# A fused attention, expert and gated-layer kernel: the embedding norm on another engine, gates and post steps at other places, a note per step in the gated layer

## The chip, the cores and the metric

The kernel runs on one core of one Trainium2 chip. The metric is the device time of one execution in microseconds (us); of several executions the median counts. The five engines of the core that appear in the profile are TensorE (PE; its weight loads, which overlap its products, are PEld), VectorE (DVE), ScalarE (ACT), GpSimd (POOL) and SyncE (SP), which issues most loads and stores.

## The reference

Three layers follow one another. The first is a recurrent attention over 4 batches, 8 heads, 768 places and 40 columns per head:

```python
for t in range(S):
    m_new = np.maximum(f_gate[:, :, t] + m, i_gate[:, :, t])
    f_stab = np.exp(f_gate[:, :, t] + m - m_new)
    i_stab = np.exp(i_gate[:, :, t] - m_new)
    m = m_new
    C = f_stab * C + i_stab * outer(v[t], k[t])
    n = f_stab * n + i_stab * k[t]
    y[:, :, t] = sigmoid(o_gate[t]) * (C @ q[t]) / np.maximum(np.abs(n @ q[t]), 1.0)
```

Its 3072 rows of 320 columns go through eight experts, of which each row takes the one with the largest logit:

```python
xn = x / (norm(x) + 1e-06)
en = expert_emb / (norm(expert_emb) + 1e-06)
logits = xn @ en.T / tau
expert_idx = np.argmax(logits, axis=1)
out[mask] = gate_w[mask, None] * (np.maximum(x[mask] @ w1[e], 0.0) @ w2[e])
```

The rows then go through a gated layer with 1536 hidden columns: `(sigmoid(x @ w_gate) * (x @ w_val)) @ w_out`. `expert_emb` has 8 rows of 320 columns; its norm, and the factor 1/tau with it, is what the change moves.

## The kernel before, in words

**Order.** The program sets the order itself: each engine runs its instructions in the order in which the code issues them, and a wait is a wait for everything behind it on that engine. `weave` issues several lists of operations in turn, one of each. `sideq` is a queue of small VectorE operations, and `side(n)` issues the next n of it at the place where it stands.

**Attention stage (to about 146 us).** There are 24 tiles, numbered from 0: tile i is chunk i // 4 (128 places) of batch i % 4. A tile passes through these steps:

- `st_S` (L428): TensorE's eight score products into two banks (`s_ps`); from tile 9 on every other tile (`HALF`) uses half of the rows only. VectorE masks both banks (`am`, and `s_ps` in place), ScalarE casts both to `ah`, GpSimd and VectorE form the remainders `al`. The first callable that it gets runs between the products and the masks, the second ahead of VectorE's `al`.
- `st_V` and `st_V2`: GpSimd scales the values with the gate column `w_all` (`vw`), ScalarE casts them to `vh`, GpSimd forms `vl`.
- `st_AV`: TensorE multiplies scores and values into bank 4 (`o_ps`); from chunk 1 on four products with the state `cst` stand ahead.
- `st_U`: TensorE's state update into bank 5 (`u_ps`); ScalarE (chunk 0) or VectorE adds it to `cst`.
- `post_ops`: VectorE's `den` (three operations) and `x`, ScalarE's sigmoid, GpSimd's product `x` and a copy.
- `st_XT` and `st_logit`: TensorE's transposes of `x` (`tp_x`), and its products with the embeddings (`l_ps`), which VectorE copies to `rs`.

The loads are issued by SyncE in the program's order; there are five buffers for keys and values (`kv`) and six for queries (`qk`), and a load waits until the tile before in its buffer is done.

**Gates.** `gate_ops(lo, hi)` is a chain of six VectorE operations on 32 rows, two of them scans; `st_gexp` takes ScalarE's exponentials, and `st_gates2` transposes both on TensorE (`tp_r`) and writes the columns `w_all` and `ri_all`. Chunk 0 has its gates ahead of tile 0, chunk 1 in the first tiles, chunks 2 to 5 together: their VectorE operations stand between tiles 5 and 8, and the exponentials and transposes of the loop's step `GX` = 5 and 6. The transposes of chunks 2 to 5 use bank 5, which the state updates use too.

**Embedding norm.** `emb_norm` squares the embeddings on ScalarE (L308), takes the root by three Newton steps on VectorE (`sqrt_ops`, L161 to L165, one column of 8 rows), and scales the embeddings on VectorE (L314). Its 15 VectorE operations come from `sideq`: `early(i)` weaves four or five of them between the post operations of the tiles 0 to 2. `emb_T` transposes the scaled embeddings after tile 5's scores.

**Filler products.** `warm(n)` issues n products of 128 x 512 ones whose result nobody reads.

**Expert stage (to about 365 us)** and **gated layer (to the end).** The gated layer runs 72 steps t, each one column block of 128 hidden columns for 512 rows. `gated_a(t)` issues the products in one half of the array's rows, gate and value products in turn into two banks; `gated_b(t)` issues those of the other halves into the same banks. So that both don't write a bank at once, `note` (L1591) lets ScalarE copy one element (`seen`) when the last product of `gated_a` is done, and `turn_rows` lets the first product of `gated_b` wait for this copy. In the steps 0 and 1 `gated_a(0)` and `gated_a(1)` are issued one after the other, and both note under the key "l1". Then ScalarE takes the sigmoid (L1622), VectorE multiplies (L1623), ScalarE casts to `hh` (L1633), GpSimd forms `hl` (L1634). `group_x` prepares the rows of the next group in three parts (`xsteps` says in which steps), each a cast on ScalarE (L209) and a subtraction on GpSimd. Beside that, pieces of weights are split on VectorE and ScalarE.

## Time and profile before

| | |
|---|---|
| three timed runs | 761.12, 763.30, 763.08 us; median 763.08 |
| the profiled execution's own time | 759.18 us, with a span of 757.4 us from its first to its last instruction |
| instructions | 17682 |
| mean granted TensorE clock | 0.993 of full speed |
| busy | PE 727.0, DVE 403.3, ACT 364.5, POOL 397.4 us |
| stages | attention to about 146 us, experts to about 365, gated layer to the end |

The rows below come from the profiled execution. In a timeline row the first number is the start in us from the span's start, the second the length in us; then come the engine, the line, the operation with its output and inputs, and how many of its kind the row merges. A bracket tells how long the engine stood idle ahead of it, and what ended that. Several short operations can overlap by their latency, so that the distance of two starts says more than the busy time.

### The profile page before, as it was taken

The numbers are of one execution on the slowest core, as the hardware profiler recorded it, in microseconds if no ns is written. First come the engines' busy times: TensorE is split into PE (matmuls) and PEld (weight loads), VectorE is DVE, ScalarE is ACT, GpSimd is POOL, SyncE is SP. The second block draws the span as 40 slices with busy tenths as digits, with TensorE's granted clock in tenths as the row PEclk, the third lists the DMA queues.
The fourth block names the chain that finished last, engine by engine and source line by source line (L and its number), as shares of the span: only waits on it lengthen the run. The fifth ranks groups of instructions, "written<-read, shape, count | busy, mean of one in ns | idle before, by whom it ended". The sixth has DMA issues, their size and how long they took to land. (4 is left out here: it accounts for less than half of the span.)

```text
span 757.4 us, 17682 instructions
## 1 busy us (share of the span) xinstructions
PE 727.0 (96%) x6906; PEld 645.3 (85%) x6906; DVE 403.3 (53%) x864; ACT 364.5 (48%) x829; POOL 397.4 (52%) x449
## 2 busy tenths in 40 slices
PE   6889999899999999999899999999999999999995
PEld 5779998799888989999688888888888888888884
DVE  7897999877778777865566664132121111111111
ACT  5765664645965656665454444333333333333322
POOL 6767887757766777886053233542324324324222
PEclk9999999999999999999999999999999999999999
DMA  7654875545455556651112210000000000000001
GB/s 221 193 160 122 265 217 162 168 119 163 146 153 160 157 158 193 185 150 53 53 57 81 81 54 19 37 35 2 1 12 27 2 1 37 1 2 35 2 1 39
DMA packets 39864, 70.46 MB, mean 93 GB/s; under 512 B 4818, under 2 KB 28460, under 8 KB 39772
## 3 DMA queue, kind: packets, MB, share of 16 engines
q1 hardware_dynamic: 36764, 59.61, 26.7%
q0 software_dynamic: 3008, 9.64, 3.9%
q8 instruction: 56, 0.92, 0.5%
q14 instruction: 36, 0.29, 0.1%
HBM read 60.55 MB, written 8.68 MB: 91 GB/s over the span
## 5 line engine op out<-in xcount | busy, mean ns | idle before, releaser
L1634 POOL TENSOR_TENSOR hl<-sgm,hh 128x512 fp32r<-128x512 f32 x71 | 95.1, 1342 | 228.5 <-ACT hh L1633 228.4
L1623 DVE TENSOR_TENSOR sgm<-v_ps,sgm 128x512 f32<-128x512 f32 (+1 forms) x73 | 49.8, 683 | 231.8 <-ACT sgm L1622 231.8
L1659 PE MATMUL o_ps<-wo,hl 64*128 64x320 f32 x560 | 87.2, 307 | 0.0
L1658 PE MATMUL o_ps<-wo,hh 64*128 64x320 f32 x560 | 86.7, 305 | 0.0
L1657 PE MATMUL o_ps<-wo,hh 64*128 64x320 f32 x560 | 86.4, 304 | 0.0
L1622 ACT ACTIVATE sgm<-g_ps 128x512 f32<-128x512 f32 (+1 forms) x73 | 43.2, 593 | 81.7 <-PE g_ps L1581 74.3
L1593 ACT COPY seen<-zeros 1x1 f32<-1x1 f32 x142 | 27.0, 190 | 105.5 <-PE v_ps L1581 57.6
L1633 ACT CAST hh<-sgm 128x512 fp32r<-128x512 f32 (+1 forms) x73 | 44.8, 615 | 48.1 <-DVE sgm L1623 47.7
L1041 ACT ACTIVATE hh<-h_ps 128x256 fp32r<-128x256 f32 (+7 forms) x72 | 35.3, 490 | 55.1 <-PE h_ps L953 50.1
L1579 PE MATMUL v_ps<-xg,wvh 64*128 64x512 f32 x144 | 56.6, 393 | 2.4 <-ACT seen L1593 2.4
L1657 PEld LDWEIGHTS o_ps<-wo,hh 64*128 64x128 f32 x560 | 53.0, 185 | 6.6 <-issue 0.3
L1658 PEld LDWEIGHTS o_ps<-wo,hh 64*128 64x128 f32 x560 | 52.8, 184 | 5.8
L1579 PE MATMUL g_ps<-xg,wgh 64*128 64x512 f32 x144 | 56.6, 393 | 0.0
L1579 PE MATMUL v_ps<-xh,wvh 64*128 64x512 f32 x144 | 56.5, 392 | 0.0
L1579 PE MATMUL g_ps<-xh,wgh 64*128 64x512 f32 x144 | 56.5, 392 | 0.0
L1580 PE MATMUL g_ps<-xg,wgh 64*128 64x512 f32 x144 | 56.4, 392 | 0.0
L1580 PE MATMUL v_ps<-xl,wvh 64*128 64x512 f32 x144 | 56.4, 392 | 0.0
L1580 PE MATMUL v_ps<-xg,wvh 64*128 64x512 f32 x144 | 56.4, 392 | 0.0
L1580 PE MATMUL g_ps<-xl,wgh 64*128 64x512 f32 x144 | 56.4, 392 | 0.0
L1581 PE MATMUL g_ps<-xg,wgl 64*128 64x512 f32 x144 | 56.2, 390 | 0.0
L1581 PE MATMUL v_ps<-xg,wvl 64*128 64x512 f32 x144 | 56.2, 390 | 0.0
L1581 PE MATMUL v_ps<-xh,wvl 64*128 64x512 f32 x144 | 56.2, 390 | 0.0
(354 smaller groups left out, 2603.8 us busy)
## 6 DMA issues: line engine op xcount, KB each, us to landing
kv<-in_kvo_dram SPq DMA_DIRECT2D x24, 484.0 KB
w2raw<-in_moe_w_dram SPq DMA_DIRECT2D x32, 320.0 KB
w1raw<-in_moe_w_dram SPq DMA_DIRECT2D x32, 256.0 KB
qk<-in_qkt_dram SPq DMA_DIRECT2D x48, 160.0 KB
xs<-x SPq DMA_DIRECT2D x24, 192.0 KB
w1raw<-in_moe_w_dram SPq DMA_DIRECT2D x64, 64.0 KB
raw<-in_moe_w_out_dram SPq DMA_DIRECT2D x12, 320.0 KB
raw<-in_moe_w_gate_dram SPq DMA_DIRECT2D x8, 384.0 KB
```

The source lines that it names most:

```text
L1041: nc.scalar.activation(out=h[f][0], in_=ps, func=AF.Relu)
L1579: lambda: nc.tensor.matmul(ps, at(wh), h[rows, kk], start=start, stop=False),
L1580: lambda: nc.tensor.matmul(ps, at(wh), l[rows, kk], start=False, stop=False),
L1581: lambda: nc.tensor.matmul(ps, at(wl), h[rows, kk], start=False, stop=stop),
L1593: passed[key] = nc.scalar.copy(seen, zeros[0:1, 0:1])
L1622: nc.scalar.activation(out=s[:, cs], in_=pg[:, cs], func=AF.Sigmoid)
L1623: nc.vector.tensor_tensor(out=s[:, cs], in0=pv[:, cs], in1=s[:, cs], op=ALU.mult)
L1633: nc.scalar.copy(gh[:, cs], s[:, cs])
L1634: e.tensor_tensor(out=gl[:, cs], in0=s[:, cs], in1=gh[:, cs], op=ALU.subtract)
L1657: lambda: nc.tensor.matmul(o, gh[rows, ts_], wh[rows], start=begin, stop=False),
L1658: lambda: nc.tensor.matmul(o, gh[rows, ts_], wl[rows], start=False, stop=False),
L1659: lambda: nc.tensor.matmul(o, gl[rows, ts_], wh[rows], start=False, stop=end),
```

## The change

- **Tile 0.** The embeddings' load is issued ahead of tile 0's keys and values. The square on ScalarE stands ahead of the first gate exponentials. VectorE's masks come ahead of the two gate columns, and the two integer operations that start the root (`norm_seed`) behind these.
- **Norm.** Of the 15 VectorE operations eleven go to GpSimd (`norm_steps`: three steps of three operations, and two more), between tile 0's `vw` and `vl`. The reciprocal stays on VectorE, between tile 1's masks and its `al`; the scaling goes to ScalarE. The transposes of the embeddings come ahead of tile 0's `tp_x`, behind tile 4's scores.
- **Post steps of tiles 0 to 3.** They are issued as the second callable of `st_S`, between the masks and `al`, not ahead of the masks.
- **Gates.** Those of chunk 1 stay where they were. Those of chunks 2 to 5 are taken from `sideq` from tile 3 on; with `GX` = 4 their exponentials and transposes come one step of the loop earlier.
- **Filler products.** Two behind the value products of tiles 1, 2 and 3, and three ahead of the first logits, where there were five.
- **Gated layer.** `note` and `turn_rows` use the step as key, a one-element sigmoid is taken ahead of step 0, and the next group's rows are prepared in the steps 2, 3 and 4, not 1, 2 and 3.

VectorE, from tile 1's `al` to tile 2's `al`, before (`sq_y`, `sq_t` and `en` belong to the norm):

```order
L455 TENSOR_TENSOR al<-s_ps,ah 128x512
L524 TENSOR_TENSOR den<-o_ps,ri_all 128x8
L155 TENSOR_SCALAR sq_y<-en_258 8x1
L527 SCALAR_TENSOR_TENSOR den<-o_ps,den 128x8
L156 TENSOR_SCALAR sq_y<-sq_y 8x1
L530 RECIPROCAL den<-den 128x8
L161 TENSOR_TENSOR sq_t<-sq_y,en_258 8x1
L532 TENSOR_TENSOR x_324<-o_ps,den 128x320
L162 SCALAR_TENSOR_TENSOR sq_t<-sq_t,sq_y 8x1
L447 TENSOR_TENSOR am<-s_ps,cmask 128x512
L449 TENSOR_TENSOR s_ps<-s_ps,cmask 128x512
L455 TENSOR_TENSOR al<-s_ps,ah 128x512
```

and changed:

```order
L470 TENSOR_TENSOR al<-s_ps,ah 128x512
L462 TENSOR_TENSOR am<-s_ps,cmask 128x512
L464 TENSOR_TENSOR s_ps<-s_ps,cmask 128x512
L539 TENSOR_TENSOR den<-o_ps,ri_all 128x8
L542 SCALAR_TENSOR_TENSOR den<-o_ps,den 128x8
L545 RECIPROCAL den<-den 128x8
L547 TENSOR_TENSOR x_349<-o_ps,den 128x320
L470 TENSOR_TENSOR al<-s_ps,ah 128x512
```

The norm's operations are gone, and the post operations (`den`, `x`) stand behind the masks.

TensorE, behind the scores of tile 9, before (`r_ps` are the rank products, `tp_r` the gate transposes, `o_ps` with `cst` the state products):

```order
L543 MATMUL tp_x<-ident,x 128x128 x3
L484 MATMUL u_ps<-vw,kv_129 40x41 x8
L435 MATMUL s_ps<-qk_125 128x128 x8
L555 MATMUL l_ps<-enT,xt 128x8 x3
L387 MATMUL tp_r<-ident,it 128x32 x4
L387 MATMUL tp_r<-ident,ft 128x32 x4
L464 MATMUL o_ps<-cst_136,qk_123 128x82 x4
```

and changed, behind the rank products that follow tile 8's scores:

```order
L590 MATMUL r_ps<-sel,ones_bf 128x8
L594 LDWEIGHTS ones_bf
L594 MATMUL r_ps<-run,ones_bf 128x32
L400 MATMUL tp_r<-ident,it 128x32 x4
L400 MATMUL tp_r<-ident,ft 128x32 x4
L479 MATMUL o_ps<-cst_135,qk_122 128x82 x4
```

The gate transposes moved one tile ahead.

ScalarE at the start of the gated layer, before (`seen` are the notes, `fa` and `wo` belong to the splitting of weights, `xh` to the next group's rows):

```order
L1593 COPY seen<-zeros 1x1 x2
L1112 ACTIVATE fa<-fa,relu_b 128x320
L1095 CAST wo<-fb 128x320
L1622 ACT_TABLE_LOAD
L1622 ACTIVATE sgm<-g_ps 128x512
L1633 CAST hh<-sgm 128x512
L1112 ACTIVATE fa<-fa,relu_b 128x320
L1622 ACTIVATE sgm<-g_ps 128x512
L1095 CAST wo<-fb 128x320
L1633 CAST hh<-sgm 128x512
L209 CAST xh<-yT 128x512
L1593 COPY seen<-zeros 1x1 x2
```

and changed:

```order
L1743 ACT_TABLE_LOAD
L1743 ACTIVATE dum<-zeros 128x1
L1615 COPY seen<-zeros 1x1 x2
L1134 ACTIVATE fa<-fa,relu_b 128x320
L1117 CAST wo<-fb 128x320
L1644 ACTIVATE sgm<-g_ps 128x512
L1655 CAST hh<-sgm 128x512
L1134 ACTIVATE fa<-fa,relu_b 128x320
L1644 ACTIVATE sgm<-g_ps 128x512
L1117 CAST wo<-fb 128x320
L1655 CAST hh<-sgm 128x512
L1615 COPY seen<-zeros 1x1 x2
```

The table load (with the one-element sigmoid `dum`) came to the front, and the cast of `xh` is gone from in front of the second pair of notes.

The diff, cut to its core:

```diff
-    def emb_norm():
-        esq = ap_.tile([NE, DM], F32, name="esq")
-        en1 = ap_.tile([NE, 4], F32, name="en1")
-        return [
-            lambda: nc.scalar.activation(out=esq, in_=eb, func=AF.Square, accum_out=en1[:, 0:1])
-        ] + sqrt_ops(ap_, en1[:, 1:2], en1[:, 0:1]) + [
-            lambda: nc.vector.tensor_scalar(
-                out=en1[:, 2:3], in0=en1[:, 1:2], scalar1=1e-6, scalar2=tb, op0=ALU.add, op1=ALU.mult
-            ),
-            lambda: nc.vector.reciprocal(en1[:, 3:4], en1[:, 2:3]),
-            lambda: nc.vector.tensor_scalar_mul(eb, eb, en1[:, 3:4]),
-        ]
+    esq = ap_.tile([NE, DM], F32, name="esq")
+    en1 = ap_.tile([NE, 4], F32, name="en1")
+    en_sq, en_y, en_t, en_r = (en1[:, j:j + 1] for j in range(4))
+    def norm_seed():
+        yi = en_y.bitcast(I32)
+        nc.vector.tensor_single_scalar(out=yi, in_=en_sq.bitcast(I32), scalar=1, op=ALU.logical_shift_right)
+        nc.vector.tensor_scalar(
+            out=yi, in0=yi, scalar1=-1.0, scalar2=float(0x5F3759DF), op0=ALU.mult, op1=ALU.add
+        )
+    def norm_steps():
+        g = nc.gpsimd
+        two = lambda o, x, u, w, op0, op1: g.tensor_scalar(out=o, in0=x, scalar1=u, scalar2=w, op0=op0, op1=op1)
+        for _ in range(3):
+            two(en_t, en_y, en_sq, en_y, ALU.mult, ALU.mult)
+            two(en_t, en_t, -0.5, 1.5, ALU.mult, ALU.add)
+            g.tensor_tensor(out=en_y, in0=en_t, in1=en_y, op=ALU.mult)
+        g.tensor_tensor(out=en_y, in0=en_y, in1=en_sq, op=ALU.mult)
+        two(en_t, en_y, 1e-6, tb, ALU.add, ALU.mult)
+    def norm_scale():
+        nc.vector.reciprocal(en_r, en_t)
+        nc.scalar.activation(out=eb, in_=eb, func=AF.Copy, scale=en_r)
...
             load_qk(j)
+        if j == 0:
+            nc.sync.dma_start(out=eb, in_=emb)
         load_kv(j)
         if j == 1:
-            nc.sync.dma_start(out=eb, in_=emb)
             nc.sync.dma_start(out=tb, in_=tau.rearrange("(a b) -> a b", a=1).to_broadcast([NE, 1]))
...
             )
-        nc.vector.tensor_copy(enT[:, 0:2].rearrange("p a b -> p (a b)"), tp[:, 0:2 * NE])
-        nc.vector.tensor_copy(enT[0:RM, 2], tp[0:RM, 2 * NE:3 * NE])
+        return [
+            lambda: nc.vector.tensor_copy(enT[:, 0:2].rearrange("p a b -> p (a b)"), tp[:, 0:2 * NE]),
+            lambda: nc.vector.tensor_copy(enT[0:RM, 2], tp[0:RM, 2 * NE:3 * NE]),
+        ]
...
+    nc.scalar.activation(out=esq, in_=eb, func=AF.Square, accum_out=en_sq)
     for op in gate_ops(0, L):
...
     st_gexp(0, L)
-    st_S(0, lambda: st_gates2(0, 1))
+    st_S(0, None, lambda: (st_gates2(0, 1), norm_seed()))
     def load(i):
...
-    def early(i):
-        st_AV(i)
+    def first_post(i):
         post[i] = post_ops(i)
-        weave(post[i][0:3] + post[i][4:5], [side] * 4)
-    sideq += gate_ops(L, 2 * L)
+        weave(post[i][0:3] + post[i][4:5])
     st_V(0)
-    side(6)
+    norm_steps()
+    weave(gate_ops(L, 2 * L))
     st_V2(0)
-    sideq += emb_norm()
-    side(1)
     act_zero(qk[0])
     st_gexp(L, 2 * L)
-    st_S(1)
+    st_S(1, None, norm_scale)
     st_V(1)
     st_V(2)
-    st_S(2, lambda: (early(0), st_V2(1)))
+    st_S(2, lambda: (st_AV(0), st_V2(1)), lambda: first_post(0))
     load(4)
...
     post[0][5]()
-    st_S(3, lambda: early(1))
+    st_S(3, lambda: (st_AV(1), warm(2)), lambda: first_post(1))
     st_U(1)
     st_V2(3)
-    side(2)
     post[1][5]()
     load(5)
-    st_S(4, lambda: (st_XT(0), early(2), side(len(sideq))))
+    sideq += gate_ops(2 * L, S)
+    side(1)
+    turned = []
+    st_S(
+        4, lambda: (turned.extend(emb_T()), st_XT(0), st_AV(2), warm(2)),
+        lambda: (weave(turned), first_post(2)),
+    )
     st_sig(2)
...
     post[2][5]()
+    side(1)
     st_V(4)
     st_U(2)
-    st_S(5, lambda: (st_XT(1), emb_T(), st_AV(3), st_post(3)))
-    sideq += gate_ops(2 * L, S)
-    GX = 5
+    st_S(5, lambda: (st_XT(1), st_AV(3), warm(2)), lambda: st_post(3))
+    side(1)
+    GX = 4
     for i in range(3, NTILE - B):
...
             st_V2(i + 1)
+            if i == GX + 1:
+                st_gexp(2 * L, S)
             post = post_ops(i)
...
         else:
-            warm(5)
+            warm(3)
             st_logit(0)
...
                 add()
+            if i == 3:
+                st_logit(1)
             st_logit(i - 1)
-        then = (lambda: st_logit(1)) if i == 3 else first_rows if i == NTILE - B - 1 else None
-        st_S(i + NAHEAD, then, between)
+        st_S(i + NAHEAD, first_rows if i == NTILE - B - 1 else None, between)
         if i > B and i % B == 1:
...
             st_sig(GX + 1)
-            st_gexp(2 * L, S)
         if i == 8:
...
             ins = woven(*(products(r, ps, w, xg[g], kk, fs) for r, ps, w in zip(halves, gv[t], gate_val)))
-        note(ins[-1], "l1")
+        note(ins[-1], t)
...
             ))
-            if kk == 0 and "l1" in passed:
-                turn_rows(ins[0], "l1")
+            if kk == 0:
+                turn_rows(ins[0], t)
         pg, pv = gv.pop(t)
...
     allj = range(G4)
-    xsteps = {1 + u: (1, u) for u in range(3)}
+    xsteps = {2 + u: (1, u) for u in range(3)}
     xsteps.update({order2.index((1, 6)) + 2 * u: (2, u) for u in range(3)})
...
         if t == 0:
+            nc.scalar.activation(out=dum, in_=zeros[:, 0:1], func=AF.Sigmoid)
             gated_a(0)
```

## Rows read from the trace of the kernel before

**Rows 1.** Page, part 1: busy us (share of the span) and instructions of each engine.
```profile
PE 727.0 (96%) x6906; PEld 645.3 (85%) x6906; DVE 403.3 (53%) x864; ACT 364.5 (48%) x829; POOL 397.4 (52%) x449
```

**Rows 2.** TensorE's waits from 200 us on: total, times, longest.
```profile
PE v_ps L1579 <- ACT seen L1593: 2.4, 2, 2.0
...
PE g_ps L1579 <- ACT sgm L1622: 0.3, 1, 0.3
```

**Rows 3.** Timeline of VectorE, tile 0: start, length, operation, [idle before <- releaser].
```profile
5.58 0.43 DVE L359 TENSOR_TENSOR_SCAN mt<-ft,it 32x128 f32<-32x128 f32 x1 [1.37 <-DMA it<-in_i_gate_dram]
...
8.53 0.19 DVE L389 TENSOR_SCALAR w_all<-tp_r 128x32 f32<-128x32 f32 x1 [0.94 <-PE tp_r L387]
...
10.73 0.69 DVE L455 TENSOR_TENSOR al<-s_ps,ah 128x512 f16<-128x512 f32 x1 [0.71 <-ACT ah L450]
```

**Rows 4.** Timeline of VectorE, tiles 1 to 4, and the post step of tile 8.
```profile
20.33 0.69 DVE L455 TENSOR_TENSOR al<-s_ps,ah 128x512 f16<-128x512 f32 x1 [0.71 <-ACT ah L450]
...
21.13 0.16 DVE L524 TENSOR_TENSOR den<-o_ps,ri_all 128x8 f32<-128x8 f32 x1
...
23.96 0.67 DVE L447 TENSOR_TENSOR am<-s_ps,cmask 128x512 f32<-128x512 f32 x1
...
26.55 0.14 DVE L161 TENSOR_TENSOR sq_t<-sq_y,en 8x1 f32<-8x1 f32 x1
...
29.02 0.67 DVE L447 TENSOR_TENSOR am<-s_ps,cmask 128x512 f32<-128x512 f32 x1
...
30.95 0.69 DVE L455 TENSOR_TENSOR al<-s_ps,ah 128x512 f16<-128x512 f32 x1 [0.65 <-ACT ah L450]
...
66.34 0.16 DVE L524 TENSOR_TENSOR den<-o_ps,ri_all 128x8 f32<-128x8 f32 x1
...
67.45 0.28 DVE L607 TENSOR_TENSOR oh_b<-ob,tv 128x128 bf16<-128x128 f32 x1
```

**Rows 5.** Timeline of TensorE, tiles 4 to 9: scores and state products.
```profile
34.22 2.05 PE L435 MATMUL s_ps<-qk 128*128 128x128 f32 x16
...
37.37 1.10 PE L464 MATMUL o_ps<-cst,qk 128*128 128x82 f32 x8
...
42.68 1.10 PE L464 MATMUL o_ps<-cst,qk 128*128 128x82 f32 x8
...
53.51 1.16 PE L435 MATMUL s_ps<-qk 40*128 40x128 f32 x16
```

**Rows 6.** Timeline of VectorE, from tile 8's first mask to tile 10's.
```profile
50.43 0.67 DVE L447 TENSOR_TENSOR am<-s_ps,cmask 128x512 f32<-128x512 f32 x1
...
51.63 0.65 DVE L495 SCALAR_TENSOR_TENSOR cst<-u_ps,cst 40x164 f32<-40x164 f32 x2
...
60.28 0.17 DVE L524 TENSOR_TENSOR den<-o_ps,ri_all 128x8 f32<-128x8 f32 x1 [1.82 <-PE o_ps L473]
...
63.64 0.69 DVE L447 TENSOR_TENSOR am<-s_ps,cmask 128x512 f32<-128x512 f32 x1 [1.17 <-POOL vl L419]
```

**Rows 7.** Timeline of ScalarE, the first sigmoids of the attention stage.
```profile
21.32 1.28 ACT L504 ACT_TABLE_LOAD   x1
22.61 0.83 ACT L504 ACTIVATE kv<-kv 128x320 f32<-128x320 f32 x2
```

**Rows 8.** Timeline of TensorE, the gate transposes of chunks 2 to 5.
```profile
56.82 0.40 PE L387 MATMUL tp_r<-ident,it 32*128 32x32 f32 x4 [0.42 <-DVE cst L495]
57.06 0.41 PE L387 MATMUL tp_r<-ident,ft 32*128 32x32 f32 x4
```

**Rows 9.** Timeline of ScalarE, first steps of the gated layer.
```profile
371.18 1.28 ACT L1622 ACT_TABLE_LOAD   x1
...
378.35 0.61 ACT L209 CAST xh<-yT 128x512 fp32r<-128x512 f32 x1
```

**Rows 10.** Timeline of GpSimd, four additions of eight columns.
```profile
52.95 1.04 POOL L583 TENSOR_TENSOR run<-run,sel 128x8 bf16<-128x8 bf16 x4
```

**Rows 11.** Windows: us, busy of PE, PEld, DVE, ACT, POOL, PEclk, DMA share, GB/s.
```profile
20.00:30.00 10.00, 7.24 (x89) 6.71 (x89) 8.90 (x27) 6.76 (x16) 6.52 (x9) 0.83 0.50 134
```

## The prediction

> **What bounds the kernel now.** I read the busy shares first [rows 1]: TensorE works 96% of the span, so only places where it waits can give time back. The list of TensorE's waits after 200 us has 3.7 us in all; 2.9 of them lie in the first three steps of the gated layer [rows 2], two kinds of 2.4 and 0.3 us and one wait of 0.2. So the expert stage and the gated layer are TensorE at work, and a new order can pay at two places: the head of the attention stage and the first steps of the gated layer. There I read the timeline, engine by engine.
>
> In the head it is VectorE's chain. Once the gate scan can start at 5.58 (it waits for a load), VectorE has one long wait, 0.94 us for TensorE's transposes of the gates [rows 3], and then no idle time up to 58 us but one short wait per tile, in front of `al`, which needs ScalarE's cast `ah` (0.71 us in tiles 0 and 2, 0.65 in tile 4) [rows 3, 4]. In tiles 1 and 2 the embedding norm's one-column operations lie between the operations of the post step: from their first operation to the next mask pass 2.83 us in tile 1 and 2.47 in tile 2, where tile 8's post step, alone, takes 1.11 [rows 4]. From tile 4 on TensorE is nearly as full: from one state product to the next a tile takes 5.31 us with no idle time, of which the scores are 2.05, or 1.16 in tiles that use half of the rows [rows 5]. The tiles 8 to 10 then have two long waits on VectorE, 1.82 and 1.17 us [rows 6].
>
> **The change part by part**, as it moves the first mask of tile 10, now at 63.64 [rows 6], since from there both orders issue the same work.
>
> (a) Tile 0. The masks stand ahead of the two gate columns, so they start when the gate scan ends, not after the transposes. The wait of 0.94 goes, and the two column writes (0.19 busy, about 0.1 apart) move into the wait of 0.71 in front of `al` [rows 3], with the two seed operations of the norm. Gain 1.1; between 0.7 (if the square on ScalarE, now ahead of the gates' exponentials, waits for its load) and 1.2. That load is issued right behind the gate loads, which landed by 5.58 [rows 3].
>
> (b) The norm leaves VectorE's post steps: (2.83 - 1.11) + (2.47 - 1.11) = 3.1 us [rows 4]. The reciprocal that stays goes into tile 1's wait in front of `al` and costs nothing. Ends: 2.0, if the stretched operations among them were stretched by GpSimd's work and other ones take their place, and 3.3 with the few in tile 0's post step.
>
> (c) The post step (1.11) of tiles 0 to 3 now lies between the masks and `al` of tiles 2 to 5 and covers the four waits there: 2 x 0.71 + 2 x 0.65 = 2.7 [rows 4], where two of the four stand. Ends 1.3 (half are covered) and 2.7.
>
> (d) A new wait. ScalarE loads the sigmoid table behind the casts of tile 2, 1.28 us, and runs two sigmoids, 0.83 [rows 7]. Now VectorE reaches tile 3's first mask only at 23.96 [rows 4], when they are over. With what (a) to (c) give until then, and its post step moved behind the masks, it comes there near 19.1 and wants `al` at 21.5. ScalarE, still behind tile 2's casts, starts the load at about 19.3, is free at 21.4 and has cast tile 3 at 22.6. Cost 1.15; ends 0 (hidden as now) and 2.1 (all of it).
>
> In this place a page speaks another way. The Trainium skill, "ScalarE: Activation LUTs", section "What ACT_TABLE_LOAD costs", gives 1283 ns for the load and a drain of some 1380 ns behind it, 2.66 us for a switch. Here the sigmoid starts at 22.61, the moment the load of 21.32 ends [rows 7]; no drain shows. By the page (d) would be about 2.5 and the total 1.4 less.
>
> (e) The gates of chunks 2 to 5. Their six operations are done before tile 8's masks in both orders, so (a) to (d), 5.75 us, hold at that point. Their exponentials and transposes now come one tile earlier, and tile 8's weights no longer wait for them. From tile 8's mask to tile 10's pass 13.21 us [rows 6]. VectorE's waits in it are 3.0, but TensorE won't let it have them all. Its own work is two tiles less the half-row scores of tile 9, 2 x 5.31 - (2.05 - 1.16) = 9.7 [rows 5], and the transposes, 0.6 [rows 8]. These use the bank of the state update, whose last reader is VectorE's `cst` addition, 51.63 + 0.65 - 50.43 = 1.85 us behind the mask [rows 6]; TensorE has only logits and ranks to do meanwhile, so I give it 1.2 idle. In sum 11.5 to 11.6; gain 1.6, with 0 and 3.0 as ends. This new wait holds the state products of tile 6 behind it, and they VectorE's post step.
>
> The filler products (2, 2 and 5 in place of 5) stand where TensorE waits for GpSimd's `x`, so I cost them at nothing; without that cover four more are under 1 us.
>
> (f) The gated layer. TensorE waits 2.0 us in step 2 and 0.3 in step 0 for ScalarE's one-element copy that notes the end of the other rows' products [rows 2]. In step 0 the note of step 1 was waited for; with a note per step that goes. The table load of 1.28 stands in front of the first sigmoid, and the cast of the next group's tokens (start to next start 0.52) in front of step 2's note [rows 9]. The chain from first sigmoid over VectorE to step 2's note leads here, so both come off: 1.8 us. Ends: 0.3, if VectorE's splitting of weights leads instead, and all waits, 2.9.
>
> (g) GpSimd takes eleven one-column operations between tile 0's `vw` and `vl`. It has no such row; the nearest are the additions of 8 columns, 1.04 for four, 0.26 each [rows 10]: 2.9 us. Behind `vw`, which I place at 10.8, they end near 13.7; VectorE's reciprocal wants them at 14.6, and TensorE reads `vl` first at about 15. So they cost nothing; at 0.6 each they would hold VectorE by 2.7 us, which is the low end.
>
> Here the Trainium skill speaks against the change: "GPSIMD Engine Reference", section "4.1 Engine selection", wants elementwise work on VectorE, GpSimd being about twice as slow for two inputs. Applied to the 0.28 us that each of the eleven norm operations in tiles 1 and 2 adds on VectorE (3.1 / 11), that is an estimate of 0.56 each, 6.2 in all, and a reciprocal 2.4 late; the total would be 6.8.
>
> The sum is 1.1 + 3.1 + 2.7 - 1.15 + 1.6 + 1.8 = 9.15 us. The profiled execution took 759.18 (span 757.4), so it would be 750.0; it is 3.9 below the median of the runs shown. Taken from that median, 763.08, the change comes to **753.9 us**.
>
> **Rivals.**
>
> 1. Half of it: GpSimd's chain or the stretched gate operations hold VectorE, the table load shows in full, and TensorE's bank wait eats (e). The low ends with half of (b) and (c): 0.7 + 2.0 + 1.3 - 2.1 + 0 + 1.8 = 3.7, so 759.4. For it: every engine is between 5 and 10 tenths busy there. Against: the waits that vanish are plain in the rows.
>
> 2. More: TensorE alone sets the head and no note is waited for: 1.1 + 3.1 + 2.7 + 3.0 + 2.9 = 12.8, so 750.3. Against: the table load has nowhere to hide.
>
> 3. Nothing: the order moves but the loads don't come sooner, and by tile 10 the gain is given back: 763. Loads are issued in order by SyncE when a tile frees its buffer. Against: from 20 to 30 us the DMA engines were busy half of the time [rows 11].
>
> 4. Slower, by TensorE's clock. From 20 to 30 us the granted clock was 0.83 [rows 11]: part of that stretch ran at 1.2 in place of 2.4 GHz, behind waits of about 1 us in front of the state updates. In the new order TensorE is done with its part earlier and then stands in front of GpSimd's `x`. If the clock stays at the lower level over the tiles 3 to 5, three tiles of 5.31 [rows 5] take twice as long: + 15.9 - 9.15 = 6.8 slower, 769.8. It decides from 1.7 tiles at the lower level on. Against: nine filler products in place of five, and shorter waits.
>
> **How the numbers follow.** The forecast, a gain of 6 to 12, has 0.66; rival 1 has 0.16, rival 2 0.06, rival 3 0.06 and rival 4 0.06. A measurement of this kernel tells about 0.3%, 2.3 us, from no change. All of the forecast and rivals 1 and 2 are beyond it: faster 0.88; rival 3 is the same, 0.06; rival 4 slower, 0.06. The range for 8 in 10 goes from rival 2 to rival 1: 750.0 to 759.5; outside lie rivals 3 and 4 and the outer parts of 1 and 2.
>
> **What would show it.** Right: tile 8's first mask near 44.7 and tile 10's near 56; no wait in front of `al` in tiles 2, 4 and 5, but one of about 1 us in tile 3, with ScalarE's table load ahead; the norm's eleven rows on GpSimd done by 14; TensorE's wait for notes in the gated layer down by 0.3 to 2 us and its first step starting over 7 us sooner; a granted clock over 0.83 from 20 to 30 us. Wrong: a granted clock at the lower level over several tiles, a reciprocal that waits for GpSimd, loads that TensorE waits for in tiles 6 to 12, or a head that gains and an end of the attention stage that stays where it is.

## The result and the profile after

The change took the time from 762.10 us (median of 4 runs) to **752.96 us** (median of 4); ratio 0.9876, 95% interval 0.9855 to 0.9898. Forecast were 753.9 from 763.08, a ratio of 0.988. The profiled execution took 753.39, against 759.18 before: 5.8 us less, where the working had 9.15. So the total came out as forecast and the sum behind it did not; the experiments show part of why.

Page of the changed kernel, part 1 (before: [rows 1]):

```profile
PE 726.3 (97%) x6910; PEld 647.7 (86%) x6910; DVE 400.6 (53%) x852; ACT 365.1 (49%) x831; POOL 397.6 (53%) x460
```

VectorE in the head of the changed kernel, timeline (columns as in [rows 3]; `am` is a tile's first mask, here of the tiles 0, 3, 6, 8 and 10; `al` those of the tiles 0, 2 and 3):

```profile
5.92 0.42 DVE L372 TENSOR_TENSOR_SCAN mt<-ft,it 32x128 f32<-32x128 f32 x1 [1.71 <-DMA it<-in_i_gate_dram]
...
7.91 0.67 DVE L462 TENSOR_TENSOR am<-s_ps,cmask 128x512 f32<-128x512 f32 x1
...
9.84 0.69 DVE L470 TENSOR_TENSOR al<-s_ps,ah 128x512 f16<-128x512 f32 x1 [0.23 <-ACT ah L465]
...
15.05 0.15 DVE L326 RECIPROCAL en<-en 8x1 f32<-8x1 f32 x1 [0.77 <-POOL en L317]
...
19.24 0.69 DVE L470 TENSOR_TENSOR al<-s_ps,ah 128x512 f16<-128x512 f32 x1 [1.23 <-ACT ah L465]
...
20.05 0.68 DVE L462 TENSOR_TENSOR am<-s_ps,cmask 128x512 f32<-128x512 f32 x1
...
23.51 0.69 DVE L470 TENSOR_TENSOR al<-s_ps,ah 128x512 f16<-128x512 f32 x1 [1.15 <-ACT ah L465]
...
35.94 0.67 DVE L462 TENSOR_TENSOR am<-s_ps,cmask 128x512 f32<-128x512 f32 x1
...
45.49 0.69 DVE L462 TENSOR_TENSOR am<-s_ps,cmask 128x512 f32<-128x512 f32 x1 [1.08 <-POOL vl L434]
...
46.69 0.66 DVE L510 SCALAR_TENSOR_TENSOR cst<-u_ps,cst 40x164 f32<-40x164 f32 x2
...
59.69 0.68 DVE L462 TENSOR_TENSOR am<-s_ps,cmask 128x512 f32<-128x512 f32 x1
```

The row at 46.69 is tile 8's addition to `cst`; it is used below. Tile 0's first mask comes 1.99 us behind the first scan (before 3.16), tile 8's at 45.49 (before 50.43, forecast 44.7), tile 10's at 59.69 (before 63.64, forecast 56). So 4.9 us were gained by tile 8, and 1.0 of it was lost in the two tiles behind it, where the forecast had 1.6 more. The four waits in front of `al` in the tiles 2 to 5 are gone in 4 and 5; in tile 3 the table load stands, as forecast; in tile 2 there is a wait of 1.23 that was not.

ScalarE ahead of these two waits, timeline:

```profile
17.74 0.47 ACT L433 CAST vh<-vw 128x328 f16<-128x328 f32 x1 [1.89 <-POOL vw L424]
18.11 0.61 ACT L463 CAST ah<-am 128x512 f16<-128x512 f32 x1
...
20.23 1.28 ACT L519 ACT_TABLE_LOAD   x1
21.53 0.83 ACT L519 ACTIVATE kv<-kv 128x320 f32<-128x320 f32 x2
22.26 0.60 ACT L463 CAST ah<-am 128x512 f16<-128x512 f32 x1
```

and GpSimd, which it waits for, timeline (first and last rows of the norm's eleven operations, and what was queued behind them):

```profile
11.14 0.71 POOL L317 TENSOR_SCALAR en<-en 8x1 f32<-8x1 f32 x2
...
14.76 0.26 POOL L317 TENSOR_SCALAR en<-en,tb 8x1 f32<-8x1 f32 x1
15.09 0.81 POOL L434 TENSOR_TENSOR vl<-vw,vh 128x328 f16<-128x328 f32 x1
15.86 1.16 POOL L466 TENSOR_TENSOR al<-am,ah 128x512 f16<-128x512 f32 x1
16.98 1.43 POOL L424 TENSOR_TENSOR vw<-kv,w_all 128x328 f32<-128x328 f32 x2
```

The chain of eleven took 3.88 us (11.14 to 15.02). Behind it stood `vl` of tile 0, `al` of tile 1 and `vw` of tile 1; ScalarE's `vh` waited for that `vw` with tile 2's casts queued behind it, and VectorE's `al` waited for the casts.

TensorE: its longest wait between 20 and 70 us, and its clock behind it in windows of 1 us (columns as in [rows 11]):

```profile
47.50 0.40 PE L400 MATMUL tp_r<-ident,it 32*128 32x32 f32 x4 [1.19 <-ACT ah L463]
```

```profile
48.00:49.00 1.00, 1.00 (x9) 0.96 (x8) 1.00 (x4) 0.00 (x0) 0.92 (x3) 0.73 0.84 283
49.00:50.00 1.00, 1.00 (x17) 1.00 (x17) 0.17 (x1) 0.00 (x0) 0.84 (x4) 0.50 1.05 402
50.00:51.00 1.00, 1.00 (x19) 0.73 (x17) 0.33 (x2) 0.00 (x0) 0.40 (x1) 0.50 0.59 239
51.00:52.00 1.00, 1.00 (x7) 0.51 (x5) 0.83 (x4) 0.00 (x0) 0.00 (x0) 0.56 0.03 12
```

The bank wait of 1.2 us stands where step (e) put it, and its length is right. The bracket names ScalarE's cast `ah`, which ended at 47.48, but the transposes started 0.15 us behind the end of the addition to `cst` (47.35), and before the change, where the bracket names `cst`, 0.14 behind it; so the bank fits. ScalarE's timeline shows a second bound close by:

```profile
44.53 1.28 ACT L391 ACT_TABLE_LOAD   x1
...
46.36 0.61 ACT L392 ACTIVATE ft<-Gt 32x512 f32<-32x512 f32 x1
```

The transposes also read these exponentials, which ended at 46.97. Since TensorE stood from 46.31 on, about 0.7 of the 1.19 would be left without the bank. Behind the wait TensorE ran at 1.2 GHz for parts of four windows: 0.27 + 0.50 + 0.50 + 0.44 = 1.7 us of full speed lost.

In the gated layer one wait is left of the three [rows 2], in step 2. TensorE's and ScalarE's timelines there:

```profile
374.19 0.50 PE L1601 MATMUL v_ps<-xg,wvh 64*128 64x512 f32 x1 [1.50 <-ACT seen L1615]
```

```profile
362.95 1.28 ACT L1743 ACT_TABLE_LOAD   x1
...
373.43 0.62 ACT L1655 CAST hh<-sgm 128x512 fp32r<-128x512 f32 x1 [1.03 <-DVE sgm L1645]
373.95 0.41 ACT L1615 COPY seen<-zeros 1x1 f32<-1x1 f32 x2
```

The table load is done ahead of step 0, the next group's cast is out of the way, and what holds the note now is the cast `hh` of step 1 in front of it.

### The profile page after: what moved, and what is told of

Read it like the earlier page. It is cut to its first block, busy times and chain, and to the rows that moved or that the text cites. A ratio compares the mean times of both kernels' runs of the same rounds, so it can differ in the third digit from the quotient of the medians.

```text
span 751.7 us, 17696 instructions
## 1 busy us (share of the span) xinstructions
PE 726.3 (97%) x6910; PEld 647.7 (86%) x6910; DVE 400.6 (53%) x852; ACT 365.1 (49%) x831; POOL 397.6 (53%) x460
## 5 line engine op out<-in xcount | busy, mean ns | idle before, releaser
L1655 ACT CAST hh<-sgm 128x512 fp32r<-128x512 f32 (+1 forms) x73 | 44.8, 615 | 46.7 <-DVE sgm L1645 46.3
```

The source lines that it names most:

```text
L1655: nc.scalar.copy(gh[:, cs], s[:, cs])
```

## The experiments

The theory after the result: the head gains about what the rows promised until TensorE sets the pace, near tile 8; from there the stops of TensorE, and the stretches at 1.2 GHz behind them, decide what is kept. Its rival: only the order counts, and the clock is a thing beside it. All ratios are to the kernel before, with 95% intervals; the clock is the mean granted clock, as the median over the timed runs. In the four sets of runs it was 0.987 to 0.989 for the kernel before; for the changed one it was 0.9915.

| kernel | ratio | interval | clock |
|---|---|---|---|
| changed kernel | 0.9876 | 0.9855 to 0.9898 | 0.9915 |
| b_gated | 0.9976 | 0.9965 to 0.9988 | 0.9895 |
| b_warm | 0.9965 | 0.9953 to 0.9977 | 0.994 |
| a_fill8 | 0.9871 | 0.9849 to 0.9893 | 0.995 |
| a_nofill | 0.9897 | 0.9874 to 0.9920 | 0.9925 |
| a_dvenorm | 0.9903 | 0.9877 to 0.9929 | 0.993 |
| a_earlypost | 0.9931 | 0.9913 to 0.9948 | 0.992 |
| a_lategate | 0.9910 | 0.9891 to 0.9929 | 0.988 |
| a_tab | 0.9885 | 0.9866 to 0.9905 | 0.991 |
| a_norm2 | 0.9943 | 0.9923 to 0.9962 | 0.9865 |
| c_fillend | 0.9874 | 0.9857 to 0.9891 | 0.997 |
| c_all | 0.9859 | 0.9842 to 0.9875 | 0.997 |
| c_best | 0.9851 | 0.9822 to 0.9880 | 0.995 |

Most intervals overlap with that of the changed kernel, so what follows rests on the profiles. The first gate scan, which waits for a load, started between 5.58 and 6.91 us in these fourteen profiles, in either order; where kernels are compared by a mask, times count from that scan unless a place in the span is given.

**b_gated: the gated layer's part alone.**

```diff
-        note(ins[-1], "l1")
+        note(ins[-1], t)
...
-    xsteps = {1 + u: (1, u) for u in range(3)}
+    xsteps = {2 + u: (1, u) for u in range(3)}
...
+            nc.scalar.activation(out=dum, in_=zeros[:, 0:1], func=AF.Sigmoid)
```

> The kernel before with the gated layer's part of the change alone (a note per step, the dummy sigmoid, the next group's tokens a step later). The theory of the forecast: the table load (1.28 us) and the cast (0.52) leave the chain to step 2's note, so TensorE's wait there falls from 2.01 to about 0.2 to 1.5, the wait of 0.34 in step 0 goes, and the time is 1.8 to 2.2 us below the kernel before (ratio about 0.9975). Rival: the changed kernel's gated layer gained only because it was entered in another phase; then the waits stay near 2.0 and 0.34 and the time is that of the kernel before. The head (to 146 us) is that of before, so this run also shows how far the head of before moves between two profiled executions: theory, tile 10's first mask within 0.5 us of 63.64.

Measured: ratio 0.9976, so 1.8 us of 760.8. The waits are those of the changed kernel: none in step 0, and in step 2

```profile
381.33 0.50 PE L1579 MATMUL v_ps<-xg,wvh 64*128 64x512 f32 x1 [1.50 <-ACT seen L1593]
```

The theory holds. Its other expectation failed: the head is the same program as before, and yet tile 10's first mask came at 66.84, 3.2 later than 63.64. The scan had started 1.2 later, and from 55 to 65 us the clock was 0.54 and 0.50, where the kernel before had 0.74 and 0.92: one program, and 2 us apart by the clock alone.

**a_fill8: fillers in TensorE's wait for the bank.**

```diff
         if i == GX + 1:
+            warm(5)
             st_gates2(2, NCH)
```

> The changed kernel with five filler products on TensorE ahead of the transposes of the gates (tp_r), where it stands for 1.19 us. Theory (clock): that stop is what brings the granted clock down to 1.2 GHz from 48.3 to 51.6 us, at a cost of about 1.6 us; with fillers the clock stays at 2.4 GHz there, tile 9's first mask comes near 52.0 in place of 53.7 and tile 10's near 58.0 in place of 59.7; the time falls by about 1.6 us below the changed kernel. Rival (load): the clock falls for another reason than that stop; then the low stretch stays and the time is that of the changed kernel or up to 0.3 us more.

The wait and the slow stretch are both gone. Windows of a_fill8 and then of the changed kernel:

```profile
40.00:60.00 20.00, 19.90 (x287) 17.51 (x286) 15.89 (x46) 13.22 (x28) 14.36 (x23) 1.00 0.48 154
```

```profile
40.00:60.00 20.00, 18.81 (x250) 16.77 (x249) 14.41 (x43) 12.14 (x26) 13.23 (x21) 0.91 0.46 144
```

Tile 10's first mask came at 58.28, by the scan 1.5 before that of the changed kernel (52.22 and 53.77). The times (749.87 to 752.67) don't tell the two apart beyond the intervals; all five runs had a clock of 0.994 or 0.995, those of the changed kernel 0.988 to 0.995.

**a_nofill: without the six fillers of the tiles 3 to 5.**

```diff
-    st_S(3, lambda: (st_AV(1), warm(2)), lambda: first_post(1))
+    st_S(3, lambda: st_AV(1), lambda: first_post(1))
...
```

> The changed kernel without the filler products in tiles 3, 4 and 5 (six products; the five of the old place are put back as they were). Theory (clock): without them TensorE stands for about half a microsecond to 1 us at several places from 22 to 30 us, the granted clock of 20 to 30 us falls from 1.00 to 0.8 to 0.9 as in the kernel before, and tile 6's first mask comes 1 to 2 us later than 35.9. Rival (order): VectorE sets the pace in these tiles and the fillers only lie in idle time; then tile 6's first mask stays within 0.3 us of 35.9 and the time is that of the changed kernel.

The theory failed: the clock stayed at 1.00 from 20 to 40 us and tile 6's first mask came 30.05 us behind the scan (30.02 with the fillers). They cost nothing, as the working had it, and they bought nothing in this execution. The stops of the new order up to there were 0.37 to 0.48 us, and no lowered clock followed them.

**a_dvenorm: the eleven norm operations on VectorE.**

```diff
-        g = nc.gpsimd
+        g = nc.vector
```

> The changed kernel with the eleven one-column operations of the norm on VectorE at the same place of the program, in place of GpSimd. Theory of the forecast (GpSimd pays): VectorE takes about 11 x 0.2 = 2.2 us more in front of tile 1's masks, so tile 1's first mask comes near 15.2 in place of 13.0 and all that follows to tile 4 about 2 us later; the time is 0 to 2 us above the changed kernel, less what TensorE's own pace hides. Rival (GpSimd's chain is itself the late one): the 3.9 us that it takes there hold vl, al and the next vw on GpSimd, and with them ScalarE's casts for tile 2, where VectorE waits 1.23 us in front of al; with the chain on VectorE that wait falls to about 0.2 and tile 3's first mask comes within 1 us of 20.05, so the time is the same within 0.5 us.

First and last rows of the chain on VectorE's timeline, and the gate scan behind it:

```profile
11.41 0.43 DVE L317 TENSOR_SCALAR en<-en 8x1 f32<-8x1 f32 x2
...
13.74 0.20 DVE L317 TENSOR_SCALAR en<-en,tb 8x1 f32<-8x1 f32 x1
13.87 0.47 DVE L372 TENSOR_TENSOR_SCAN mt<-ft,mt,it 32x128 f32<-32x128 f32 x1
```

VectorE needs 2.46 us (11.41 to 13.87), 0.22 for each, GpSimd 3.88, 0.35 for each. Tile 1's first mask came 1.9 later by the scan, but the wait of 1.23 in tile 2 was 0.0, and by tile 6 only 0.7 of the 1.9 was left. At tile 10 it stood 0.7 behind a_fill8 (52.96 and 52.22), in which the clock was 1.00 too; the changed kernel, which had lost speed there, was later than both (53.77). Both halves are right: GpSimd's place is worth 0.7 us in the head, not 2.5, because its own chain comes back as the wait in tile 2.

The same run has TensorE's wait of 1.19 us in front of `tp_r`, at 49.15, and no slow stretch behind it:

```profile
40.00:60.00 20.00, 18.81 (x262) 17.17 (x263) 15.72 (x48) 13.43 (x30) 14.16 (x23) 1.00 0.48 147
```

The wait alone doesn't bring the clock down.

**a_earlypost: the post steps of tiles 0 to 3 in front of the masks.**

```diff
-    st_S(3, lambda: (st_AV(1), warm(2)), lambda: first_post(1))
+    st_S(3, lambda: (st_AV(1), warm(2), first_post(1)))
...
```

> The changed kernel with the post steps of tiles 0 to 3 back in front of the masks of tiles 2 to 5 (with the product of the next tile's start as in the kernel before). Theory of the forecast: each post step, 1.1 us, stands ahead of a mask again and the wait in front of al comes back behind it, 0.65 to 0.71 in four tiles, so tile 6's first mask comes 1.3 to 2.7 us later than 35.9. Rival (ScalarE bounds tiles 2 and 3, where VectorE waits 1.23 and 1.15 us in front of al anyway): there the post step only fills what is a wait either way, so only tiles 4 and 5 lose, 1.3 together, and since TensorE sets the pace from tile 6 on, the time moves by less than 0.5 us.

Tile 6's first mask came 1.9 us later by the scan, within the theory's range; the waits in front of `al` in the tiles 4 and 5 are back (0.65 each), that of tile 2 fell to 0.71. At tile 10 it stands only 0.4 behind the changed kernel (54.16 and 53.77), but its clock stayed at 1.00 there, where the changed kernel's did not. Against a_fill8, whose clock stayed at 1.00 too, the 1.9 is still there at tile 8 (41.44 and 39.51) and at tile 10 (54.16 and 52.22): TensorE's pace hides nothing of it, and the rival fails. The median is the one that is clearly above the changed kernel with the same clock: 0.9931, by the ratios 4.2 us more. What adds to the 1.9 there is open.

**a_lategate: exponentials and transposes of the gates one tile later.**

```diff
-    GX = 4
+    GX = 5
...
+            st_gexp(2 * L, S)
```

> The changed kernel with exponentials and transposes of the gates of chunks 2 to 5 one tile later, as in the kernel before. Theory (the earlier gates as such give nothing; they bring TensorE's wait of 1.19 us in front of tp_r and the stretch at 1.2 GHz behind it, which together eat the 3.0 us of waits that they save): with late gates tile 10's first mask comes within 1 us of 59.7 in the profile, TensorE waits for VectorE's rs and ScalarE's xt instead (1.4 and 0.9 us as in the kernel before), and the time is within 1 us of the changed kernel. Rival (the forecast's term): late gates give back 1.6 us or more, tile 10's first mask at 61.3 or later.

Tile 10 came at 60.14, by the scan 0.7 behind the changed kernel, as the theory has it, though TensorE's waits were shorter than it said (0.50 and 0.78) and the clock from 50 to 60 us was 0.66. The median lies 0.0034 above that of the changed kernel, 2.6 us; the clocks, 0.988 and 0.9915, account for as much (0.0035 x 757). So the earlier gates show no gain beside the clock; how they compare at full clock comes under (e) below.

**a_tab: the sigmoid table ahead of tile 2's casts.**

```diff
     st_S(1, None, norm_scale)
+    st_sig(0)
+    st_sig(1)
...
```

> The changed kernel with ScalarE's first two sigmoids, and with them the load of the sigmoid table, moved ahead of tile 2's casts, where ScalarE stood for 1.89 us waiting for GpSimd's vw (15.85 to 17.74). Theory (the table load is what tile 3's al waits for): the wait of 1.15 in front of tile 3's al goes, tile 2's casts are at most 0.3 later, and tile 4's first mask comes 0.8 to 1.2 us earlier than 25.35; since TensorE's wait for tp_r and its pace stand behind that, 0 to 1 of it reaches the end. Rival (ScalarE is full either way): tile 2's wait in front of al grows by what tile 3's loses, and tile 4's first mask stays at 25.35 within 0.3.

Tile 3's `al` no longer waits and comes 1.1 us earlier by the scan; tile 4's first mask gains only 0.2. That is the rival's number without its reason, since tile 2's wait grew only from 1.23 to 1.36. VectorE between them, timeline:

```profile
22.10 0.68 DVE L470 TENSOR_TENSOR al<-s_ps,ah 128x512 f16<-128x512 f32 x1
22.70 2.23 DVE L372 TENSOR_TENSOR_SCAN mt<-ft,mt,it 32x512 f32<-32x512 f32 x1
24.86 0.65 DVE L462 TENSOR_TENSOR am<-s_ps,cmask 128x512 f32<-128x512 f32 x1
```

GpSimd beside it:

```profile
22.70 1.16 POOL L466 TENSOR_TENSOR al<-am,ah 128x512 f16<-128x512 f32 x1
23.82 1.72 POOL L434 TENSOR_TENSOR vl<-vw,vh 128x328 f16<-128x328 f32 x1
```

The scan of 512 columns took 2.23 us. In the changed kernel, where it began when GpSimd's `al` was nearly done, it took 1.31, and the `vl` of the same place took 1.48 in place of 1.72:

```profile
23.20 1.16 POOL L466 TENSOR_TENSOR al<-am,ah 128x512 f16<-128x512 f32 x1
24.56 1.48 POOL L434 TENSOR_TENSOR vl<-vw,vh 128x328 f16<-128x328 f32 x1 [0.21 <-ACT vh L433]
```

So 0.92 of the 1.1 that `al` had gained went into a longer scan, which neither expectation had. c_all and c_best, with the same edit, show the same scan (2.24 and 2.23).

**a_norm2: the norm behind tile 1's `vw`.**

```diff
-    norm_steps()
...
     st_V(1)
+    norm_steps()
...
```

> The changed kernel with GpSimd's eleven norm operations (3.9 us from 11.14 to 15.02) behind tile 1's vw in place of tile 0's, and the reciprocal and the scaling two tiles later. Theory (the chain holds GpSimd's vl and vw, and through ScalarE's cast vh, which waits for vw, the casts of tile 2's masks): vw of tile 1 is done 3 us earlier, the wait of 1.23 in front of tile 2's al falls under 0.3, and tile 3's first mask comes about 1 us earlier than 20.05; the norm then delays vl of tile 1 and TensorE's first products of tile 1 instead. Rival (GpSimd has no slack either way): what tile 2 gains is lost in tile 3, and tile 4's first mask stays at 25.35 within 0.3.

Tile 2's wait went, as the theory said. But tile 3's first mask, which should have come 1 us earlier, came 0.6 later, and tile 4's, which the rival had unmoved, 2 us later: `vl` of tile 1 was late and TensorE stood for 1.69 us at 20.6. The clock was 0.86 and 0.80 from 20 to 30 us and fell again behind the wait for `tp_r`. The place that the change gives the norm is the better one.

**b_warm: the kernel before with fillers alone.**

```diff
+    warm(4)
     st_U(1)
...
+    warm(5)
     st_U(2)
...
-            warm(2 if i < 8 else i > NTILE - B - 4)
+            warm(9 if i == 6 else 2 if i < 8 else i > NTILE - B - 4)
...
```

> The kernel before with filler products on TensorE in the six places of its head where it stands for 0.4 to 1.5 us (4 ahead of tile 1's state products, 3 ahead of tile 0's transposes, 5 ahead of tile 2's state products, and 7, 4 and 2 in the three waits from 51 to 57 us), and nothing else. Theory (a good part of the gain over the median is the clock: the change leaves TensorE fewer and shorter stops, so fewer stretches at 1.2 GHz): the granted clock of the kernel before stays at 1.00 from 20 to 70 us, the mean clock of its runs rises from 0.989 to 0.993 or more, and 2 to 4 of the 8 us that the change gains are had by fillers alone. Rival (order): the stretches at 1.2 GHz lie where VectorE sets the pace; then the clock rises and the time stays within 1 us of the kernel before.

The clock of the head stayed at 1.00, the mean clock rose from 0.989 to 0.994, and the time fell by 2.7 us (760.87 to 758.18, ratio 0.9965). From tile 8's first mask to tile 10's it took 11.75 us (51.01 to 62.76) against 13.21 [rows 6]: 1.5 us of the stretch that step (e) worked on was the clock and not the order. From 145 to 155 us its clock still fell (0.80 and 0.86 in two windows of 5 us); its fillers stand in the head alone.

**c_fillend, c_all, c_best: fillers at the end of the attention stage, and two edits more.** c_fillend has the five fillers of a_fill8, five ahead of the last logits and six ahead of the last index products. c_all adds a_tab's edit and moves ScalarE's cast of step 1 behind the note of step 2; c_best is c_all without the six.

```diff
+    fill_3(5)
     st_logit(t0 + 3)
...
+    fill_3(6)
     st_index(NTILE - 2 * B, NTILE)
...
             gated_a(t)
+            if t == 2:
+                gated_h(1, s1)
...
```

> The changed kernel with the five filler products ahead of tp_r (as in a_fill8) and, at the end of the attention stage, five ahead of the last logits (wait of 1.13 at 142.1) and six ahead of the last index products (wait of 1.42 at 149.8). Theory: the stretch at 1.2 GHz from 144 to 147.8 in the changed kernel and in a_fill8 is what follows the first of these waits; it goes, and the time is about 1 to 2 us below a_fill8 (ratio about 0.985), with a mean clock of 0.997 or more. Rival: it follows from something else there (three more profiles have it, but the kernel before, with the same wait of 1.12, does not); then it stays and the time is that of a_fill8.

> The version of c_fillend with two more edits: the first two sigmoids ahead of tile 2's casts (as in a_tab), and in the gated layer the cast of step 1's result behind the note of step 2 in place of ahead of it. Theory: tile 3's wait of 1.15 in front of al goes, of which 0.3 to 0.5 reaches tile 10 as TensorE sets the pace there; TensorE's last wait for a note, 1.50 us in step 2, falls under 0.3; together 1.5 to 2 us below c_fillend (ratio about 0.983). Rival: step 2's note is done earlier but the products behind it then wait for the cast of step 0 or 1, or for GpSimd's hl; then the wait of 1.5 moves one step down and the time is within 0.7 us of c_fillend.

> The version of c_all without the six filler products ahead of the last index products. Theory (in a_fill8 TensorE reached those products without a wait, at 148.35 where the kernel with the six fillers came at 149.66, so the fillers there stood on the path and cost their 1.3 us): the time falls by 1.0 to 1.4 us below c_all, to a ratio of about 0.984, the clock from 144 to 148 stays at 1.00, and the rest is as in c_all. Rival (TensorE waits there for VectorE's one-hot rows either way, as it did for 1.42 us in the changed kernel): the wait comes back in place of the fillers, the clock falls behind it or not, and the time is that of c_all or up to 0.5 us more.

The clock from 140 to 150 us went from 0.83 (a_fill8, changed kernel) to 1.00 in c_fillend, as expected, and the mean clock to 0.997; but the time did not fall below that of a_fill8. The last index products need rows from VectorE; they came at 148.35 in a_fill8, 149.66 in c_fillend and 149.04 in c_best, 142.29, 143.15 and 143.11 behind the scan: the full clock ahead of them brought them no sooner. The timelines show what held them. The last of VectorE's operations that they read is `oh_b`; beside it GpSimd subtracts `w1l`. In c_best and then in a_fill8:

```profile
147.53 1.38 POOL L223 TENSOR_TENSOR w1l<-w1raw,w1h 128x512 fp32r<-128x512 f32 x1 [0.86 <-ACT w1h L220]
147.70 1.28 DVE L623 TENSOR_SCALAR oh_b<-ob,pcol 128x128 bf16<-128x128 f32 x1
149.04 0.28 PE L654 MATMUL ix_ps<-oh_b,oh_p 128*128 128x64 bf16 x4 [1.44 <-DVE oh_b L623]
```

```profile
148.03 0.28 DVE L623 TENSOR_SCALAR oh_b<-ob,pcol 128x128 bf16<-128x128 f32 x1
148.35 0.41 PE L654 MATMUL ix_ps<-oh_b,oh_p 128*128 128x64 bf16 x8
148.56 1.29 POOL L223 TENSOR_TENSOR w1l<-w1raw,w1h 128x512 fp32r<-128x512 f32 x1 [1.57 <-ACT w1h L220]
```

Where `w1l` began first, `oh_b` took 1.28 and not 0.28, and TensorE waited for it, as in the changed kernel (1.42). So TensorE waited for VectorE there, and the six fillers only filled that wait. In c_all TensorE's wait of 1.50 in step 2 went; the products behind it came 1.7 us earlier than in c_fillend, but a wait of 0.39 for the next note stood in step 3, and there only 0.9 of that was left. c_best's rival held: without the six fillers the wait of 1.4 for the index products was back. c_all, at 0.9859, and c_best, at 0.9851, have the lowest ratios; that they beat the changed kernel by 1 to 2 us is likely but within the intervals.

## Why the prediction was right, and where not

**(a)** Forecast 1.1; from the first scan to tile 0's `al` it took 5.15 us before and 3.92 now: 1.2. Right.

**(b), (g)** The eleven operations don't end near 13.7, but at 15.02, since vw ended 0.3 later than placed and each took 0.35, not 0.26 (before, [rows 10]). The reciprocal waited 0.77, which the forecast had named as a sign of being wrong, and `al` behind it, whose casts were done at 14.89, came 0.2 later for it. "So they cost nothing" failed for another reason: it looked at those who read the chain's result and not at what was queued behind it on GpSimd. That cost the wait of 1.23 in tile 2, and a_dvenorm had it at 0. So of the 2.5 us that VectorE is spared, 0.7 was left. The Trainium skill, "GPSIMD Engine Reference", section "4.1 Engine selection", says that GpSimd is about twice as slow for elementwise work with two inputs. The prediction's estimate of 0.56 from it went further, since seven of the eleven operations have one input beside their scalars. For the chain of eleven the two runs show 0.35 to 0.22 us each, 1.6 times; most of the difference lies in the seven, whose pairs took 0.69 to 1.01 on GpSimd and 0.46 or 0.47 on VectorE from start to next start. The section's advice, VectorE, would have cost 0.7 us here.

**(c)** Forecast 2.7 with ends of 1.3 and 2.7; a_earlypost puts it at 1.9, at the tiles 6, 8 and 10 alike when the clock is the same. Two of the four waits went. The third is the table load's, the fourth GpSimd's.

**(d)** Forecast 1.15, seen 1.15, at the place and for the reason given. The first sigmoid starts at 21.53, the load of 1.28 having started at 20.23. The drain of some 1380 ns behind a load that the Trainium skill's page "ScalarE: Activation LUTs" gives in "What ACT_TABLE_LOAD costs" doesn't show here either. But a_tab shows that the wait's end was not its price: without it VectorE reached the next mask 0.2 us earlier.

Together (a) to (d) were forecast at 5.75 by tile 8; by the scan they came to 44.85 - 39.57 = 5.3.

**(e) failed.** "I give it 1.2 idle" was right (1.19). What the step missed first was what stood behind the wait: 1.7 us of clock. With the clock held, from tile 8's first mask to tile 10's takes 12.7 us in a_fill8 (45.57 to 58.28) and in a_dvenorm, and 14.2 in the changed kernel; forecast were 11.6. So 1.5 of the 2.6 us of error is the clock. The other 1.1 is a path that the sum did not have: it added up TensorE's work alone. In a_fill8 6.70 us pass up to tile 9's first mask, which waits for TensorE's scores; the 6.01 behind it are VectorE's own work, with one wait of 0.45.

What it missed next was its own starting point: the 13.21 held 1.5 us of lowered clock, by b_warm. With the clock at 1.00 in both orders the stretch takes 11.75 us before (b_warm) and 12.71 changed (a_fill8): not a gain of 1.6, but a loss of 1.0. a_lategate points the same way. Its clock of 0.66 from 50 to 60 us is 3.4 us of lost speed; without it tile 10 would come, by this estimate, as early as 51.1 behind the scan, and a_fill8 has 52.22. So at full clock the earlier gates seem to be worth nothing by themselves; a run of late gates with fillers, which would show it, was not made.

Rival 4 had the mechanism, but in the tiles 3 to 5 and for three tiles; it came in tile 6's products, for about 3.4 us. Filler products were put where TensorE waited in the old order; the new wait had none.

**(f)** Forecast 1.8; b_gated measures 1.8 (0.9 to 2.7), and the profile has step 2's second half at 374.19 against 379.11 with a start 2.97 earlier: 1.95. Right, with the causes named.

**What was gained and given back later.** "From there both orders issue the same work" held to 120 us (4.2 us ahead), but the changed kernel began the gated layer only 2.97 ahead, where the forecast had over 7. The lead was 4.10 at the last logits (143.20) and 3.70 at the rank products (147.27), where its clock from 140 to 150 us was 0.83 and that of the kernel before 1.00; and it fell from 3.6 to 2.97 at 177.72, where TensorE waited 0.63 for VectorE's `xl`, which it had not before.

**Why the total was right all the same: luck.** The sum was made against one execution and taken from the median of others. That execution was a fast one: its clock was 0.993, while in seventeen timed executions beside the first experiments the kernel before had 0.984 to 0.992, and 760.79 for its median. For the runs behind 763.08 and 762.10 no clock is on record. If TensorE were busy throughout, a lowered clock would take 1 - clock of the span: by this estimate 8.3 us in the median run of the kernel before and 5.3 in its profiled one, 6.4 in the median run of the changed kernel and 5.3 in its profiled one. So the clock would set the medians 1.9 us further apart than the two profiles, of the 3.4 that they are (9.14 and 5.79); the rest is open. Two errors cancelled: the sum was 3.4 too high for the execution that it was made for, and the median held about as much that no term had. Nothing in the working foresaw the second. That fillers alone, in b_warm, bring 2.7 us shows that such a part exists.

## What to carry to other kernels

Where an operation moves to an idle engine, price not only when its result is wanted but also what is queued behind it there, and who waits for that. Where a change leaves a wait of about a microsecond on TensorE, look at the granted clock behind it: the stretch at 1.2 GHz cost more than the wait in four of six profiles, and with fillers in the wait itself it was gone in four of four. Where one operation took 1.28 us in one profile and 0.28 in another, look at what its neighbour engine ran beside it. Before a sum from one profile is taken from a median, compare the profile's clock with those of the timed runs.

## What the runs showed of the hardware

Six profiles have the same wait of 1.19 us in front of the same products. It was followed by no slow stretch in two (a_dvenorm, a_earlypost), by 1.7 us of lost speed in two (changed kernel, a_nofill), and by about 6.8 in two: in a_tab the clock was 0.74, 0.50, 0.50 and 0.89 in the four windows of 5 us from 45 us on, in a_norm2 0.59, 0.50 and 0.55 in the three from 50 us on. With fillers in the wait none was seen (a_fill8, c_fillend, c_all, c_best). What chooses among them is open. The wait began at 45.8 us in a_tab, 46.3 and 46.7 in the changed kernel and a_nofill, 48.0 and 48.1 in a_dvenorm and a_earlypost, and 49.3 in a_norm2, so its time alone does not order them.

VectorE's operations were longer beside some of GpSimd's. `oh_b` (128x128) took 1.28 or 1.29 us in the eight profiles in which GpSimd's subtraction `w1l` (128x512) had begun 0.15 to 0.18 before it, and ended 0.1 or less behind `w1l`; it took 0.28 in the six in which `w1l` began later. The scan of 512 columns took 2.23 or 2.24 us in the three profiles in which it began with GpSimd's `al` (128x512), and 1.31 in the changed kernel. In a_norm2 it began 0.16 before that `al`: the scan took 1.27, and `al` took 2.07 in place of 1.16. So where one of the two had clearly begun before the other, the later one was the longer.
